# Gate/up as pairs of 64-row tiles that swap roles, in a segmented attention and feed-forward kernel

## The chip, the cores and the metric

The kernel runs on one core of a Trainium2 chip. The metric is the device time of one launch in microseconds (us). The engines of the core are named as in the profile: PE (TensorE, the matmul array) with PEld for its weight loads, DVE (VectorE), ACT (ScalarE), POOL (GpSimd), and SP, whose queue issues most of the transfers. A transfer issued by ScalarE stands on the queue ACTq.

## The reference

```python
xn = _layernorm(x)                       # x: 2048 x 448
# A: 16 heads of 28, 4 segments of 512 tokens, a memory M, z carried along
q, k, v = xn @ wq, xn @ wk, xn @ wv
for s in range(4):
    a_dot = softmax(qs @ ks.T * scale + mask) @ vs
    a_mem = (phi(qs) @ M) / (phi(qs) @ z + 1e-06)
    o = g * a_mem + (1 - g) * a_dot      # g = sigmoid(beta), one per head
    M, z = M + phi(ks).T @ vs, z + phi(ks).sum(rows)
s = o @ wo
# B: 448 -> 1792 -> 448
b = (gelu(xn @ w_gate) * (xn @ w_up)) @ w_down
out = x + s * silu(b)
```

`phi(t)` is `t + 1` for positive `t` and `exp(t)` otherwise.

## The kernel before

The work is cut into four segments of 512 tokens (four blocks of 128). The width 448 is three chunks of 128 and a rest of 64 rows; the 1792 hidden features are 14 chunks of 128 (`NFC`).

**A planner writes the order.** `fast_path` (L339) doesn't issue instructions at once. It makes a list of operations (`Op`, L26), each with its engine, a modelled duration, what it depends on (`deps`), what must have started before it (`after`), the buffers it takes (`acq`) and uses, and a priority. `arrange` (L276) plays them through on its model and sorts them by start. Each engine then executes its operations in that order. Priorities come from the table `PRIO` (L87); `STEP` (L258) says, for many operations, after which of the ten score steps of an attention they may start. Thus a change of these tables moves work on every engine, without changing the work.

**The array's modes.** The planner knows four modes of the array: full (128 rows), `r64` (two tiles of 64 rows), `r32` (four tiles of 32 rows, for the scores, L985) and `c32` (four tiles of 32 columns, for the product of probabilities and values, L1047). Tiles of one mode work side by side.

**Stages.** In order of time: normalisation of segment 0 and its projections; gate/up of segment 0 (G0); attention of segments 0 and 1 (A0, A1); G1; A2; G2; A3; G3; and the last down products (D3). The projections of later segments (L714), the down products (L1155), the memory's update and reads (L860, L898) and the output products (L1185) are fitted between the score steps.

**Gate/up** (`gate_up`, L1075). For each chunk of 128 hidden features the gate and the up product each need three full-array matmuls of 512 columns and one of 64 rows. The 64-row rests of both weights lie in one tile, `wh_sb`, gate in rows 0 to 63 and up in rows 64 to 127, so the two rests run side by side in `r64`. They are collected: `VISITS` (L1073) gives four visits a segment, in which the rests of up to four chunks are multiplied (L1104), with the full matmuls (L1089) of the chunks between the visits. Then ScalarE takes the gelu of the gate (L1114) and VectorE multiplies by the up product (L1119). A chunk holds two of the eight PSUM banks.

**Projections of later segments** (`project`, L801). Two blocks make a pair: six full matmuls as two operations (`Unit.full`, L721) and one visit in `r64` for the two 64-row rests (`visit`, L768), named `wr...`. The visit is tied to come before a given score step.

**The start** (`layer_norm(0)`, L603). All four blocks of x are centred (`xc`, L663), transposed by TensorE (L596) and evicted, and the projections of segment 0 are made from centred x; their eviction multiplies by the reciprocal width (L752, L754). The fully normalised x (L653) is transposed as well, for gate/up. ScalarE issues one x load and three loads of `wv` (L490) ahead of its first table load (L567).

**Other parts named below.** The phi exponentials of keys and queries (L826, `exwk..`, `exwq..`). The guard (L1239): squares of `wq` and `wk` (L1248), summed (L1251) into the tile `um`, one product (L1258), and comparisons; it says whether the fast path's softmax without a maximum was allowed. The same tile `um` takes the masked memory update of segments 1 and 2 (L872). The residual sum (L1176) is the last reader of x. `x_sb` has four buffers, one for each segment, `pt` (the probabilities) has five.

## Time and profile before

| | |
|---|---|
| runs, us | 229.61, 230.47, 435.18 |
| median of the runs, us | 230.47 |
| span of the profiled execution, us | 227.6 |
| mean granted clock of the array | 0.999 |
| G0 | 16.03 to 38.66 |
| A0 and A1 | 38.66 to 88.49 |
| G1 | 88.49 to 111.31 |
| A2 | 111.31 to 138.86 |
| G2 | 138.86 to 161.69 |
| A3 | 161.69 to 186.32 |
| G3 | 186.32 to 209.20 |
| D3 and the end | 209.20 to 227.60 |

The profiled execution's own time is its span of 227.6 us and what lies around it; the two lower runs are 2.0 and 2.9 us over that span. In the profile, "L1089" is line 1089 of the kernel; a group of instructions is given as output<-inputs, with partitions x elements, "x12" is the number of instructions, and an arrow in brackets names what ended the idle time before an instruction. `pp` and `ps` are PSUM banks. Starts are in us from the start of the span. Matmuls overlap, so the pitch of a row of matmuls is read from their starts or from a merged piece of the chain, not from the duration of one.

### The profile page before, as it was taken

The page shows a single profiled execution, that of the slowest core. Times are in us where ns is not written, and L with a number is a line of the kernel's source. Part 1 is how long each engine was busy: PE and PEld are TensorE (multiplying, and loading weights), DVE is VectorE, ACT ScalarE, POOL GpSimd, SP SyncE. Part 2 cuts the span into 40 slices and gives each one's busy share as a digit, 9 for nine tenths or more (in the row PEclk, how much of TensorE's full clock was granted, in tenths as well). Part 3 has the DMA queues.
Part 4 walks back from the last instruction along what each step waited for, and adds up shares of the span by engine and source line. Part 5 has one row for each costly group of instructions (what it writes and reads, how often), then busy time and mean ns, then how long its engine had stood idle before and what let it go on. Part 6 is the DMA issues. An engine that isn't in the chain of part 4 may idle for free.

```text
span 227.6 us, 4462 instructions
## 1 busy us (share of the span) xinstructions
PE 217.5 (96%) x1557; PEld 95.6 (42%) x1570; DVE 152.7 (67%) x287; ACT 152.7 (67%) x212; POOL 129.3 (57%) x221
## 2 busy tenths in 40 slices
PE   7999999889999999999999999999999999999991
PEld 2544433333544434344444444344444434444561
DVE  3799998767965795674875587863746463647262
ACT  4799645999898779432788898443878875346120
POOL 8601400579588599603599989853199477604500
PEclk9999999999999999999999999999999999999999
DMA  6999569964434763217603132272500018135011
GB/s 215 222 357 259 103 152 248 237 128 83 48 72 72 183 127 74 76 38 201 186 20 68 27 71 69 59 196 59 140 1 4 12 45 225 31 84 125 4 40 50
DMA packets 44708, 25.11 MB, mean 110 GB/s; under 512 B 30808, under 2 KB 40856, under 8 KB 44680
## 3 DMA queue, kind: packets, MB, share of 16 engines
q1 hardware_dynamic: 43704, 24.05, 44.7%
q10 hardware_dynamic: 976, 0.71, 1.0%
q8 instruction: 14, 0.23, 0.4%
q14 instruction: 14, 0.11, 0.2%
HBM read 16.00 MB, written 2.98 MB: 83 GB/s over the span
## 4 chain that ended last, share of the span: by engine, by line
PE 82%; ACT 10%; DVE 2%; issue 2%; ACTq 1%; POOL 1%; DVEq 0%; POOLq 0%
PE ps L1155 16%; PE ps L1089 15%; PE pp L1089 14%; PE ps L714 11%; PE pp L985 5%; PE ps L1185 5%; PE ps L1047 4%; ACT pt L1000 3%; PE ps L1104 3%; PE pp L1104 3%; PE pp L1155 2%; ACT pt L1248 2%; PE ps L898 1%; PE ps L860 1%; PE ps L1221 1%
## 5 line engine op out<-in xcount | busy, mean ns | idle before, releaser
L1000 ACT ACTIVATE pt<-pp 128x1024 bf16<-128x1024 f32 x75 | 73.3, 1037 | 11.8 <-PE pp L985 9.9
L1011 POOL TENSOR_SCALAR_AFFINE_SELECT pt<-pt 128x256 bf16<-128x256 bf16 x128 | 54.3, 448 | 26.0 <-ACT pt L1000 23.6
L1155 PE MATMUL ps<-wd_sb,hT 128*128 128x448 bf16 x182 | 39.0, 354 | 0.4 <-DVE qs L750 0.4
L1114 ACT ACTIVATE gl<-pp 128x512 bf16<-128x512 f32 x28 | 15.8, 595 | 29.0 <-PE pp L1104 23.2
L1155 PEld LDWEIGHTS <-hT 128*128 128x128 bf16 x210 | 18.8, 98 | 20.1 <-issue 5.0
L1119 DVE TENSOR_TENSOR hT<-gl,pp 128x512 bf16<-128x512 bf16 x28 | 18.4, 682 | 11.6 <-ACT gl L1114 11.5
L1119 DVE TENSOR_TENSOR hT<-gl,ps 128x512 bf16<-128x512 bf16 x28 | 18.7, 677 | 11.0 <-ACT gl L1114 8.4
L1114 ACT ACTIVATE gl<-ps 128x512 bf16<-128x512 f32 x28 | 16.6, 597 | 13.0 <-PE ps L1089 6.1
L1089 PEld LDWEIGHTS <-wu_sb 128*128 128x128 bf16 x168 | 16.4, 98 | 20.1 <-issue 0.3
L1089 PEld LDWEIGHTS <-wg_sb 128*128 128x128 bf16 x168 | 14.9, 98 | 22.5 <-issue 7.1
L909 POOL TENSOR_TENSOR om<-om,rb 128x512 f32<-128x512 f32 x12 | 14.9, 1268 | 15.9 <-DMA rb<-rdr 15.8
L714 PEld LDWEIGHTS <-xnT 128*128 128x128 bf16 (+1 forms) x192 | 15.0, 96 | 20.6 <-issue 10.1
L1089 PE MATMUL pp<-xnT,wu_sb 128*128 128x512 bf16 x84 | 22.7, 379 | 0.3
L1089 PE MATMUL ps<-xnT,wu_sb 128*128 128x512 bf16 x83 | 22.5, 379 | 0.2
L956 POOL TENSOR_TENSOR oT<-oa,om 128x512 bf16<-128x512 f32 x12 | 16.0, 1337 | 11.5 <-DVE oa L953 11.5
L1089 PE MATMUL ps<-xnT,wg_sb 128*128 128x512 bf16 x81 | 22.1, 380 | 0.3 <-issue 0.3
L1089 PE MATMUL pp<-xnT,wg_sb 128*128 128x512 bf16 x76 | 21.2, 380 | 0.4 <-issue 0.3
L831 POOL TENSOR_SCALAR e<-e 128x896 bf16<-128x896 bf16 (+1 forms) x12 | 12.8, 1070 | 10.9 <-ACT e L826 10.9
L985 PE MATMUL pp<-qT,kT 32*128 32x512 bf16 (+3 forms) x238 | 17.0, 301 | 2.0 <-ACT pt L1000 1.8
L646 POOL TENSOR_TENSOR rs<-rs,nhalf 128x1 f32<-128x1 f32 (+1 forms) x7 | 6.1, 882 | 16.1 <-DVE rs L641 16.1
L883 DVE COPY oa<-ps 128x512 f32<-128x512 f32 x16 | 10.9, 683 | 5.2 <-PE ps L1047 5.0
L1176 POOL TENSOR_TENSOR oo<-sg,x_sb 128x448 bf16<-128x448 f32 x12 | 12.4, 1037 | 2.7 <-DVE sg L1196 2.7
(121 smaller groups left out, 325.3 us busy)
## 6 DMA issues: line engine op xcount, KB each, us to landing
rb<-rdr SPq DMA_DIRECT2D x28, 256.0 KB
out_dram<-oo SPq DMA_DIRECT2D x15, 112.0 KB
wd_sb<-in_B_w_down_dram SPq DMA_DIRECT2D x2, 784.0 KB
x_sb<-in_A_x_dram SPq DMA_DIRECT2D x3, 448.0 KB
rdr<-dc SPq DMA_DIRECT2D x28, 32.0 KB
wg_sb<-in_B_w_gate_dram SPq DMA_DIRECT2D x2, 384.0 KB
wu_sb<-in_B_w_up_dram SPq DMA_DIRECT2D x2, 384.0 KB
wg_sb<-in_B_w_gate_dram SPq DMA_DIRECT2D x1, 576.0 KB
```

The source lines that it names most:

```text
L714: nc.tensor.matmul(out=self.bank.ap()[:, 0:D], lhsT=self.xT.ap()[r, c, n * P:(n + 1) * P], rhs=self.w[r, c, :], **kw)
L831: o = gps(f"mi{nm}{s}{half}", n / 1024, lambda: nc.gpsimd.tensor_scalar(out=t(), in0=t(), scalar1=1.0, scalar2=0.0, op0=ALU.min, op1=ALU.max),
L909: oU[s, g, 1] = t, gps(f"sm{s}{g}", 1.22, lambda t=t, r=r: nc.gpsimd.tensor_tensor(out=t.ap(), in0=t.ap(), in1=r.ap(), op=ALU.mult), deps= ...
L956: oT[s][1].append(gps(f"cb{s}{g}", 1.22, lambda g=g, t=t, tm=tm: nc.gpsimd.tensor_tensor(out=dst.ap()[:, g, :], in0=t.ap(), in1=tm.ap(), o ...
L985: nc.tensor.matmul(out=S2[i // 2].ap(i % 2)[:, c0:c0 + n], lhsT=kT[s][0].ap()[r, g, kb * P:(kb + 1) * P], rhs=qT[s][0].ap()[r, g, kb * P:L ...
L1000: nc.scalar.activation(out=dst, in_=src, func=ACT.Exp, scale=scale)
L1011: nc.gpsimd.affine_select(out=v, in_=v, pattern=[[0, 2], [1, P]], compare_op=ALU.is_ge, fill=0.0, base=0, channel_multiplier=-1)
L1089: nc.tensor.matmul(out=bf[fc].ap(i), lhsT=w[:, c, fc * P:(fc + 1) * P], rhs=xT.ap()[:, c, :], start=begins and c == 0, stop=not begins and ...
L1104: nc.tensor.matmul(out=bf[fc].ap(i), lhsT=wh_sb[r, fc * P:(fc + 1) * P], rhs=xT.ap()[r, NC3, :], start=fc in begins, stop=fc in ends)
L1114: a = act(f"ge{s}{fc}", L, lambda: nc.scalar.activation(out=gl.ap(), in_=bf[fc].ap(0), func=ACT.Gelu_apprx_tanh), func="gelu", deps=[o], a ...
L1119: nc.vector.tensor_tensor(out=hT[s][0].ap()[:, fc, :], in0=gl.ap(), in1=bf[fc].ap(1), op=ALU.mult), deps=[a] + held,
L1155: nc.tensor.matmul(out=bank.ap()[:, 0:D], lhsT=hT[s][0].ap()[:, fc, b * P:(b + 1) * P], rhs=wd_sb[:, fc, :], start=(fc == 0), stop=(fc == ...
```

## The change

Gate/up no longer uses the full array. Per chunk, `part(fc, 0)` multiplies gate weights of rows 0 to 63 and up weights of rows 64 to 127 of each of the three chunks, and the rests, as four pairs of 64-row tiles; `part(fc, 1)` swaps the roles in three pairs. Both tiles then write the other one's bank, and a tiny ScalarE activation (`ty`) between the two parts waits for both tiles of the first part and is waited for by both of the second. The order is: first part of chunk fc + 1, second part of chunk fc.

A projection pair is one operation `pj`, with its rests ahead or behind as the array's mode suggests (`flex`). In segment 0 only blocks 0 and 2 are projected from centred x (`EARLY`), the others from normalised x, and two keep-warm matmuls are added. The loads of the 64-row rests of `wv` move from ScalarE's queue to SP's. x has three buffers, so segment 3's x takes that of segment 0 after its last residual sum; `pt` has six. The masked update `um` depends on the guard. Phi exponentials of all segments may be tied to score steps, also to those of the attention before. `PRIO`, `STEP`, some modelled durations, and the choices of banks (`BANKS`) are new.

```diff
-        VISITS = (((), (0, 1)), ((2, 3), (4, 5)), ((6, 7), (8, 9)), ((10, 11), (12, 13)))
...
+            if rest:
+                prev = visit(f"wr2{s}", list(rest), at(ph, -1), after=[att.get("sc_end")])
+            def part(fc, turn):
                 nonlocal prev
 
                 def mm():
-                    for i, w in enumerate((wg_sb, wu_sb)):
-                        for c in range(NC3):
...
+                    for c in range(NC3 + 1 - turn):
                         for i in range(2):
...
+                            w = wh_sb if c == NC3 else (wg_sb, wu_sb)[i ^ turn][:, c, :]
+                            m = nc.tensor.matmul(out=bf[fc].ap(i ^ turn), lhsT=w[side[i], fc * P:(fc + 1) * P],
+                                                 rhs=xT.ap()[side[i], c, :], start=not turn and c == 0,
+                                                 stop=turn == 1 and c == NC3 - 1)
+                            if not turn:
+                                ended[fc, i] = m
+                            elif c == 0:
+                                ordered(m, turns[fc])
...
+                if not turn:
+                    def turn_over():
+                        turns[fc] = nc.scalar.activation(out=idle[0:1, :], in_=nhalf[0:1, 0:1], func=ACT.Identity)
+                        for i in range(2):
+                            ordered(turns[fc], ended[fc, i])
+                    swapped[fc] = op(f"ty{s}{fc}", {"ACT": (0.2, 0.25)}, turn_over, deps=[prev], after=[nhalf_in], prio=at(ph, fc) - 401)
...
+            part(0, 0)
+            for fc in range(NFC):
+                if fc < NFC - 1:
+                    part(fc + 1, 0)
+                h = part(fc, 1)
+                a = hidden(fc, h)
```

```diff
-        xs = tiles(NSEG, [P, NB, D], BF16, "x_sb")
+        x_p = slots(NSEG - 1, [P, NB, D], BF16, "x_sb")
+        xb = [Buf(x_p, [(s % (NSEG - 1),)]) for s in range(NSEG)]
...
-        pt_p = slots(5, [P, HG, L], BF16, "pt")
+        pt_p = slots(6, [P, HG, L], BF16, "pt")
...
-        wv_in = weight("ACT", "wv", wv_sb, A_wv)
-        wk_in = weight("SP", "wk", wk_sb, A_wk)
-        wq_in = weight("SP", "wq", wq_sb, A_wq)
+        wv_in = whole("ACT", "wv", wv_sb, A_wv)
+        wk_in = whole("SP", "wk", wk_sb, A_wk)
+        wv_in += rest("wv", wv_sb, A_wv)
+        wk_in += rest("wk", wk_sb, A_wk)
+        wq_in = whole("SP", "wq", wq_sb, A_wq) + rest("wq", wq_sb, A_wq)
...
-            out=igate[:, 0:1], in_=nhalf[:, 0:1], func=ACT.Exp), deps=[nhalf_in], after=wv_in, prio=-400)
+            out=igate[:, 0:1], in_=nhalf[:, 0:1], func=ACT.Exp), deps=[nhalf_in], after=wv_in[:1], prio=-400)
...
-                for b in range(NB):
+                for b in EARLY:
...
+                    o = turned_by_pe("c", b, [centred] + xc_z, cols, [], xcT[0], -905 + b)
+                    bank = Buf(B_, EIGHT)
+                    kept_warm.append(pe(f"wm{b}", [L], lambda bank=bank: nc.tensor.matmul(
+                        out=bank.ap(), lhsT=warm[:, 0:P], rhs=warm, start=True, stop=True), deps=[warm_in], after=[o],
+                        prio=-300 + b, acq=[bank]))
...
-                self.scaled = s == 0
+                self.scaled = s == 0 and n in EARLY
...
+                    first = o_of[us[0]].tail_first
+                    if first:
+                        tails(True)
+                    for u in us:
+                        for c in range(NC3):
+                            u.product(c, start=not first and c == 0, stop=first and c == NC3 - 1)
+                    if not first:
+                        tails(False)
...
-                    out=um[:], in0=uv(), in1=bd, op=ALU.mult), deps=[o, mem["acc"]], prio=pr - 400,
+                    out=um[:], in0=uv(), in1=bd, op=ALU.mult), deps=[o, mem["acc"], mem["ok"]], prio=pr - 400,
```

Of the tables, the prediction speaks of these entries: in `STEP`, `wo00`, `wo01`, `wo02`, `wo03` go from 10, 10, 10, 0 to 6, 7, 0, 7, and `exwk01` gets 1; in `PRIO`, `ty22` is 625 and `ge21` is 626 (the lower goes first).

More of the change, by code (lines that the diff above doesn't have):

```diff
@@ L807, in project, with mm, tails @@
                 us = [Unit(s, nm, n, -8400.0) for nm, n in pair]
[L808 to L813 removed]
+                def mm(us=us):
+                    def tails(first):
+                        for u in us:
+                            u.product(NC3, start=first, stop=not first)
+                    first = o_of[us[0]].tail_first
+                    if first:
+                        tails(True)
+                    for u in us:
+                        for c in range(NC3):
+                            u.product(c, start=not first and c == 0, stop=first and c == NC3 - 1)
+                    if not first:
+                        tails(False)
+                u, nm = us[0], pair[0][0]
+                new = not u.dst[2:] and nm != "wq"
+                ns = [D] * (2 * NC3 + 1)
+                occ = sum(n / 2400 + 0.0025 for n in ns) + SWITCH
+                o = op("pj{}{}{}".format(s, *pair[0]), {"PE": (occ, occ + 0.17)}, mm, mode="full", flex=True,
+                       deps=sum((x.needs(False) + x.needs(True) for x in us), []), prio=-8400.0,
+                       acq=[x.bank for x in us] + ([u.dst[0]] if new else []), uses=[u.xT], after=u.dst[2:3])
+                o_of[u] = o
+                if new:
+                    u.dst.append(o)
+                for x in us:
+                    x.out(o)
+                pairs_of.append((o, sc, k))
+        o_of, pairs_of = {}, []
         tabled, phis = [], []
@@ L1071, in fast_path, with ordered @@
         hT = {}
-        VISITS = (((), (0, 1)), ((2, 3), (4, 5)), ((6, 7), (8, 9)), ((10, 11), (12, 13)))
+        def ordered(later, earlier):
+            tc.add_manual_dep(later.ins, earlier.ins.name, mybir.DependencyInfo(
+                mybir.DependencyClass.Sync, mybir.DependencyReason.DATA), reason="one PSUM bank, two row tiles")
         def gate_up(s, ph, rest=()):
```

156 lines of the change are left out of this document (70 added, 86 removed), and 375 rows, old and new, of tables (BANKS, PRIO, STEP).

## The prediction

> **What bounds the kernel now.** I read the page first (busy shares, then the chain that ended last), then busy time by stage, then the chain in order of time, then the waits. The page:
>
> ```profile
> PE 217.5 (96%) x1557; PEld 95.6 (42%) x1570; DVE 152.7 (67%) x287; ACT 152.7 (67%) x212; POOL 129.3 (57%) x221
> PE 82%; ACT 10%; DVE 2%; issue 2%; ACTq 1%; POOL 1%; DVEq 0%; POOLq 0%
> ```
>
> TensorE is busy in 96% of the 227.6 us, and 82% of the chain that sets the end is TensorE. A busy TensorE isn't yet one at its peak, so the question is what its time consists of. By stage (gate/up of segment 0, attention of segments 0 and 1, gate/up of 1, of 2, of 3):
>
> ```profile
> core 0: us, PE busy (x) PEld busy (x) DVE busy (x) ACT busy (x) POOL busy (x), PEclk, DMA share, GB/s
> ...
> 16.03:38.66 22.63, 22.30 (x114) 8.91 (x115) 21.45 (x51) 15.01 (x24) 3.66 (x3) 1.00 0.89 197
> 38.66:88.49 49.83, 47.98 (x447) 20.87 (x447) 38.17 (x73) 44.70 (x56) 37.98 (x72) 1.00 0.61 117
> 88.49:111.31 22.82, 22.56 (x130) 9.30 (x132) 13.88 (x22) 11.15 (x18) 11.04 (x13) 1.00 0.47 122
> ...
> 138.86:161.69 22.83, 22.57 (x131) 9.22 (x132) 14.26 (x21) 11.56 (x18) 12.86 (x14) 1.00 0.42 115
> ...
> 186.32:209.20 22.88, 22.57 (x127) 9.49 (x130) 11.18 (x19) 11.15 (x17) 10.31 (x13) 1.00 0.44 118
> ```
>
> Each gate/up stage takes 22.6 to 22.9 us with TensorE full, at granted clock 1.00, and ScalarE half idle (11 to 15 us of about 23). Attention of segments 0 and 1 has both full: TensorE 47.98 and ScalarE 44.70 of 49.83. A piece of the chain in the last gate/up stage shows what the full TensorE spends:
>
> ```profile
> 196.69 2.59 PE pp L1089 x12
> 199.28 0.54 PE pp L1104 x4
> 199.82 0.43 PE ps L1104 x4
> 200.25 2.70 PE ps L1089 x12
> ```
>
> Twelve full-array matmuls of 512 columns take 2.59, so 0.216 each. Four 64-row matmuls take 0.43: two run at a time, and a pair costs 0.216 as well. The piece in which the array goes from full to 64 rows is 0.11 longer (0.54 against 0.43), and so is the one in which it goes back (2.70 against 2.59).
>
> **The change, part by part.** *Gate/up in 64-row tiles.* Per chunk of 128 features, before: six full matmuls and one 64-row pair, 7 slots of 0.216. After: four pairs, then three pairs, again 7 slots. The streaming is unchanged at 98 slots, 21.2 us per segment. What goes are changes of mode: four visits a segment (VISITS), entered three times from full matmuls and left four times to them, so 7 x 4 = 28 changes of 0.11: -3.1 us. Coming into and leaving the stage costs as before, and so does a probability product (1047) within it. The guard's one-row product (1258) is in full mode and may now stand within 64-row work: +0.1, one change more.
>
> *Twice the instructions.* 14 matmuls a chunk for 8, 336 more in all. The same visit seen matmul by matmul:
>
> ```profile
> 199.21 0.61 PE L1104 MATMUL pp<-xnT,wh_sb 64*128 64x512 bf16 x4
> 199.65 0.59 PE L1104 MATMUL ps<-xnT,wh_sb 64*128 64x512 bf16 x4
> ```
>
> The first two pairs take 0.44 from start to start, 0.01 more than 2 x 0.216, because the start after a change is a little long; nothing shows 98 pairs in a row. I take no cost. The upper end is that 0.01 on each of 392 pairs, +3.9. The lower end is 0, since no row has a 512-column slot under 0.216. The Trainium skill, "TensorEngine Tiling (Array Packing)", section "Instruction Overhead", speaks against my zero: each matmul is to have some 60 cycles of overhead. With 512 columns in 0.216 that is an estimated 25 ns, 336 x 25 ns = 8.4 us, and the sum would be about +5 in place of -3.4; by that rule the four matmuls of 0.43 would take 0.05 longer than two full ones, which they don't, so I weigh it little.
>
> *The swap.* Between the two turns of a chunk stands a tiny ScalarE activation that waits for both tiles and that the second turn waits for.
>
> ```profile
> L1104 PE MATMUL pp<-xnT,wh_sb x56: 376/376/387, 16.0 to 205.7; 64*128 64x512 bf16 x56
> ```
>
> ```profile
> 183.45 0.39 PE L985 MATMUL pp<-qT,kT 32*128 32x512 bf16 x4
> 183.94 1.94 ACT L1000 ACTIVATE pt<-pp 128x1024 bf16<-128x1024 f32 x2 [0.64 <-PE pp L985]
> 185.93 0.39 PE L985 MATMUL pp<-qT,kT 32*128 32x384 bf16 x6 [0.30 <-ACT pt L1000]
> 188.36 1.28 ACT L1114 ACT_TABLE_LOAD   x1
> ```
>
> ```profile
> 4.36 0.20 ACT L567 ACTIVATE igate<-nhalf 128x1 f32<-128x1 f32 x1
> 17.15 1.14 ACT L752 ACTIVATE hT<-ps,rs 128x448 bf16<-128x448 f32 x2
> 36.82 0.60 ACT L1114 ACTIVATE gl<-ps 128x512 bf16<-128x512 f32 x1
> ```
>
> Its path: 0.16 for the matmul's tail (0.376 against a 0.216 slot), 0.10 from TensorE to ScalarE (183.84 to 183.94), 0.20 for the activation, 0.05 back (185.88 to 185.93): 0.51. Its cover: the second turn of the chunk before and the first of the chunk after, 7 slots, 1.51; 0.86 at the first chunk and 0.65 at the last. A gelu of 0.60 in front makes 1.11, still inside; an exponential (0.97 each in the row of two) about fits; a table load of 1.28 would be 0.28 too late, and that comes once at a stage's head. Cost taken: 0; ends 0 and 3 x 0.28 = +0.8 (a systematic wait is a rival below). 56 x 0.20 is 11 us more on ScalarE, 2.8 per stage that has 8 to 12 free. Identity costs no table load beside exponentials (17.15 follows one directly); beside gelus no row shows it. The Trainium skill, "ScalarE: Activation LUTs", section "Table sets", counts identity as a filler of every set; without that each swap would reload twice and nothing here would hold.
>
> *Gelu later.* Until now a chunk's gate product was complete three slots before its up product; now both end together, so the last gelu, the table load behind it and the first exponentials of the next attention come up to 0.65 later. *A phi exponential* of segment 0 (exwk01) is now held until the first scores, which takes 0.95 into the stage where ScalarE leads the chain:
>
> ```profile
> 22.00 0.95 ACT L826 ACTIVATE e<-kn 128x896 bf16<-128x896 bf16 x1
> 43.41 5.74 ACT pt L1000 x8
> PE pp L985 <- ACT pt L1000: 1.8, 3, 1.0
> ```
>
> There TensorE waits 1.8 us. Against it stand a sixth pt buffer and newly ordered work. Ends: all 1.8 gone, or 0.65 + 0.95 = 1.6 more. I take +0.3, near zero and on the side of the two mechanisms that I can see. After the later gate/up stages other matmuls cover it.
>
> *The start.*
>
> ```profile
> 1.33 1.70 ACTq L490 DMA_DIRECT2D wv_sb<-in_A_wv_dram  x3
> 3.06 1.28 ACT L567 ACT_TABLE_LOAD   x1 [3.06 <-issue]
> 4.46 0.56 ACT L615 ACTIVATE hT<-x_sb 128x448 bf16<-128x448 bf16 x1
> 5.58 1.05 ACT L598 COPY xnT<-ps 128x512 bf16<-128x512 bf16 x2
> 6.20 0.74 PE L714 MATMUL ps<-wv_sb,xnT 128*128 128x448 bf16 x3 [0.20 <-ACT xnT L598]
> 6.78 0.39 PE L596 MATMUL ps<-oT,hT 128*128 128x128 bf16 x4
> 7.00 0.39 PE L596 MATMUL pp<-oT,hT 128*128 128x128 bf16 x4
> 9.73 0.74 PE L714 MATMUL pp<-wk_sb,xnT 128*128 128x448 bf16 x3
> ```
>
> ScalarE issues three weight loads before its table load; two of them move to SP's queue, so its statistics and the first eviction come up to 1.1 earlier (two thirds of 1.70), and the first product at 6.20 with them. Two groups of four transposes go (0.22 each, 6.78 to 7.00): -0.44; two keep-warm matmuls come: +0.43. But only two blocks can now be projected early; the other two need their width first, and the key weights, which were used from 9.73, stand no earlier. SP issues the same two tails later, ahead of wq. Ends -1.1 and +0.5; I take -0.4.
>
> *Projection pairs as one piece, tails first or last.* A tail costs a change of 0.11 in and one out either way; only where a full product followed the tail, and scores preceded the piece, is one saved. Of 18 pairs I count that for a few: -0.3, ends -0.6 and +0.6 (the uninterrupted piece is 1.4 long and can hold scores up).
>
> *Three x buffers.* x of segment 3 now loads only after segment 0's last residual sum. *Guard:* `um` of segment 1 waits for the guard.
>
> ```profile
> 113.30 1.04 POOL L1176 TENSOR_TENSOR oo<-sg,x_sb 128x448 bf16<-128x448 f32 x1 [2.41 <-DVE sg L1196]
> 116.72 1.43 PE ps L714 x8
> 31.98 0.38 PE L1258 MATMUL ps<-um,ones 128*1 128x128 f32 x2
> 78.82 0.68 DVE L872 TENSOR_TENSOR um<-ps,bdmask 128x512 f32<-128x512 f32 x1
> ```
>
> The guard has 47 us of room: nothing. For x, a residual sum of segment 0 stood at 113.30 and segment 3's first products at 116.72, so the old order would be too late; the new steps put `wo00`, `wo01`, `wo03` after score step 6 or 7 of segment 1 (before: 10, 10, 0), some 20 us before. The load, norm and four transposes then lie in gate/up of segment 1, where VectorE is busy 13.88 of 22.82. Cost 0; if it is late, up to two product pairs of 1.43 leave attention 2 for a place among 64-row work: +0.4 for four changes, and SP's later loads of reciprocals wait behind it.
>
> Sum: -3.1 + 0.1 + 0.3 - 0.4 - 0.3 = -3.4, a span of 224.2. The runs shown are 229.61 and 230.47 (the median), 2.0 to 2.9 over the span of 227.6; with the middle, 2.45, the time is 226.7.
>
> **The rivals.** *The whole replan works* (A): the start gains its 1.1, the pairs 0.6, the waits on exponentials 1.0: -3.0 - 1.1 - 0.6 - 1.0 = -5.7, 224.4. For it: those are the only other losses on a full TensorE. Against: ScalarE at 44.70 of 49.83 leaves little. *The gain is given back in attention* (B): stages 0 and 1 get 1.6 more and pairs cost 0.6 more: -3.0 + 2.2, 229.3. For it: ScalarE's load there and the later gelu. *The swap waits* (C), the slower side: a swap queued on ScalarE behind the gelu of the chunk before, which itself waits for that chunk's second turn, comes 0.65 + 0.16 + 0.10 + 0.60 + 0.20 + 0.05 = 1.76 after its first turn against a cover of 1.51, so TensorE stands 0.25. At 14 of 56 chunks the gain is gone; at 30 the time is 226.7 + 7.5 = 234.2. Against it: the listed priorities put ty22 (625) ahead of ge21 (626). *The pace falls* (D): 0.01 more on every pair, +3.9, 230.6. For it: no row has more than four pairs in a row. Against it: within those four the pace is back to 0.216 after the first.
>
> **How the numbers follow.** Forecast 0.48, A 0.27, B 0.09, C 0.10, D 0.06. The forecast's own range is 225.0 to 228.3. The range 223.5 to 231.5 takes in A, B and D and leaves out most of C. Two per cent is 4.6 us, about what a measurement of this kernel can tell from no change: faster means under 225.9, which holds most of A and the low edge of the forecast, 0.30; slower means over 235.1, which is C with 34 or more late swaps, 0.08; the rest, 0.62, lies within.
>
> **What would show it.** Right: four gate/up stages of about 22.0 us without full-array matmuls, the two turns 0.86 and 0.65 long, no wait of TensorE for the tiny activation; the first value product before 6.0. Wrong: a wait of a gate/up product on ScalarE in the list of waits (C); 28 matmuls of two chunks taking over 3.05 (D); a longer chain through the exponentials after 40 us (B); segment 3's first products after 125 us (x late).

## The result and the profile after

The changed kernel ("after") takes 231.58 us in the median against 230.25 for the kernel before in the same rounds, a ratio of 1.0068 with a 95% interval of 1.0045 to 1.0091. It is a little slower (0.7%, and the interval is only 0.5 us to either side), where 226.7 was forecast; the time lies 0.1 above the top of the range. Ratios below are all to the kernel before, run on the same chip, and leave disturbed executions out. The profiled execution has a span of 230.1 us, 2.5 more than before. The medians differ by 1.3 only: a run lasts 1.7 to 1.9 us longer than its own span, so the profiled execution of before was about 0.9 faster than its median run, and that of after about 0.3 slower. The stage differences below are those of two single executions. First the page's busy shares and the shares of its chain:

```profile
PE 218.5 (95%) x1899; PEld 99.8 (43%) x1900; DVE 156.7 (68%) x282; ACT 164.5 (71%) x272; POOL 127.0 (55%) x221
PE 66%; DVE 12%; ACT 7%; DMA 6%; issue 4%; POOL 3%; SPq 2%; DVEq 0%; ACTq 0%
```

TensorE is still busy 95% of the span, but its share of the chain has fallen from 82% to 66%, and VectorE's has risen from 2% to 12%. That second line is the first hint. The windows by stage (start, G0, A0 and A1, G1, A2, G2, A3, G3, the end) say where:

```profile
0.00:17.12 17.12, 14.93 (x82) 6.71 (x84) 10.79 (x28) 10.68 (x22) 8.30 (x34) 1.00 0.87 263
17.12:39.03 21.91, 21.60 (x198) 9.67 (x194) 19.44 (x47) 16.76 (x39) 1.65 (x2) 1.00 0.79 152
39.03:88.98 49.95, 48.34 (x432) 20.91 (x432) 36.67 (x63) 45.69 (x60) 37.85 (x71) 1.00 0.54 112
88.98:113.49 24.51, 23.31 (x229) 11.59 (x228) 20.82 (x32) 14.55 (x32) 15.90 (x19) 1.00 0.47 120
113.49:141.69 28.20, 27.58 (x235) 12.28 (x234) 21.04 (x34) 23.54 (x28) 20.87 (x36) 1.00 0.41 76
141.69:163.62 21.93, 21.93 (x217) 9.70 (x212) 12.56 (x20) 13.62 (x31) 10.06 (x13) 1.00 0.47 125
163.62:188.71 25.09, 24.90 (x212) 10.80 (x210) 16.24 (x28) 21.27 (x25) 18.42 (x35) 1.00 0.11 29
188.71:210.64 21.93, 21.93 (x219) 9.70 (x212) 10.60 (x18) 13.20 (x30) 8.62 (x11) 1.00 0.43 120
210.64:230.10 19.46, 13.95 (x102) 8.42 (x100) 8.49 (x17) 5.18 (x11) 5.30 (x4) 0.94 0.10 29
```

Against the kernel before, the stages differ by: start +1.1 (17.12 against 16.03), G0 -0.7, A0 and A1 +0.1, G1 +1.7, A2 +0.7, G2 -0.9, A3 +0.5, G3 -0.9, end +1.1; together +2.5. In G2 and G3 TensorE is busy for all of 21.93 us, the 22.0 that the prediction named. The gain is there in three of the four gate/up stages. It is lost at the start, in G1, A2 and A3, and at the end.

That the swap costs nothing is seen in a piece of G0's chain and in the list of TensorE's waits:

```profile
30.27 1.51 PE ps L1146 x14
31.78 1.51 PE pp L1146 x14
```

```profile
PE ps L1146 <- DVE oa L936: 1.2, 2, 1.0
PE pp L744 <- ACT kn L783: 0.5, 1, 0.5
PE pp L1146 <- ACT nhalf L1158: 0.3, 1, 0.3
```

Fourteen matmuls of a chunk, seven pairs, take 1.51, so 0.216 a pair over whole stages. The tiny activation (`nhalf`, L1158) is waited for once, 0.3 us. The longest wait inside gate/up is another: for VectorE's copies `oa` (L936).

### The profile page after: what moved, and what is told of

Same layout as the page of the kernel before. It is cut to its first block, busy times and chain, and to the rows that moved or that the text cites. A ratio compares the mean times of both kernels' runs of the same rounds, so it can differ in the third digit from the quotient of the medians.

```text
span 230.1 us, 5179 instructions
## 1 busy us (share of the span) xinstructions
PE 218.5 (95%) x1899; PEld 99.8 (43%) x1900; DVE 156.7 (68%) x282; ACT 164.5 (71%) x272; POOL 127.0 (55%) x221
## 4 chain that ended last, share of the span: by engine, by line
PE 66%; DVE 12%; ACT 7%; DMA 6%; issue 4%; POOL 3%; SPq 2%; DVEq 0%; ACTq 0%
PE ps L1206 14%; PE ps L1146 13%; PE pp L1146 10%; PE ps L744 10%; PE pp L1038 4%; PE ps L1100 3%; PE ps L1236 3%; DVE hT L1172 3%; DMA rb<-rdr 2%; PE pp L744 2%; DMA x_sb<-in_A_x_dram 2%; ACT pt L1053 2%; DVE dc L973 2%; PE ps L597 2%; POOL pt L1064 1%
## 5 line engine op out<-in xcount | busy, mean ns | idle before, releaser
L1053 ACT ACTIVATE pt<-pp 128x1024 bf16<-128x1024 f32 x72 | 70.5, 1034 | 12.3 <-PE pp L1038 10.3
L1064 POOL TENSOR_SCALAR_AFFINE_SELECT pt<-pt 128x256 bf16<-128x256 bf16 x128 | 52.2, 437 | 15.8 <-ACT pt L1053 15.2
L1146 PE MATMUL ps<-xnT,wu_sb 64*128 64x512 bf16 x180 | 47.7, 376 | 0.2 <-DVE oa L936 0.2
L1146 PE MATMUL ps<-xnT,wg_sb 64*128 64x512 bf16 x180 | 46.1, 376 | 1.0 <-DVE oa L936 1.0
L1206 PE MATMUL ps<-wd_sb,hT 128*128 128x448 bf16 x196 | 42.2, 353 | 0.8 <-DVE om L936 0.5
L1146 PE MATMUL pp<-xnT,wu_sb 64*128 64x512 bf16 x156 | 41.7, 376 | 0.3 <-ACT nhalf L1158 0.3
L1146 PEld LDWEIGHTS <-wu_sb 64*128 64x128 bf16 x336 | 30.6, 94 | 21.4 <-ACT nhalf L1158 2.4
L1146 PE MATMUL pp<-xnT,wg_sb 64*128 64x512 bf16 x156 | 39.8, 376 | 0.0
L1146 PEld LDWEIGHTS <-wg_sb 64*128 64x128 bf16 x336 | 30.1, 94 | 19.5 <-issue 1.9
L744 PEld LDWEIGHTS <-xnT 128*128 128x128 bf16 (+1 forms) x192 | 15.2, 96 | 22.4 <-issue 10.6
L1158 ACT ACTIVATE nhalf<-nhalf 1x1 f32<-1x1 f32 x56 | 11.1, 198 | 16.1 <-PE ps L1146 10.1
L936 DVE COPY oa<-ps 128x512 f32<-128x512 f32 x16 | 10.7, 680 | 6.9 <-PE ps L1100 6.3
```

The costliest lines, as they stand in the source:

```text
L744: nc.tensor.matmul(out=self.bank.ap()[:, 0:D], lhsT=self.xT.ap()[r, c, n * P:(n + 1) * P], rhs=self.w[r, c, :], **kw)
L1053: nc.scalar.activation(out=dst, in_=src, func=ACT.Exp, scale=scale)
L1064: nc.gpsimd.affine_select(out=v, in_=v, pattern=[[0, 2], [1, P]], compare_op=ALU.is_ge, fill=0.0, base=0, channel_multiplier=-1)
L1146: m = nc.tensor.matmul(out=bf[fc].ap(i ^ turn), lhsT=w[side[i], fc * P:(fc + 1) * P], rhs=xT.ap()[side[i], c, :], start=not turn and c == ...
L1158: turns[fc] = nc.scalar.activation(out=idle[0:1, :], in_=nhalf[0:1, 0:1], func=ACT.Identity)
L1206: nc.tensor.matmul(out=bank.ap()[:, 0:D], lhsT=hT[s][0].ap()[:, fc, b * P:(b + 1) * P], rhs=wd_sb[:, fc, :], start=(fc == 0), stop=(fc == ...
```

## Three places to look at

**G1: one short VectorE instruction.** VectorE's rows in G1, then GpSimd's of the same time:

```profile
90.44 4.00 DVE L973 TENSOR_SCALAR dc<-dc,igate 128x64 f32<-128x64 f32 x1 [0.74 <-DMA dc<-den]
94.48 0.55 DVE L977 RECIPROCAL dc<-dc 128x64 f32<-128x64 f32 x1
94.95 1.22 DVE L936 COPY oa<-ps 128x512 f32<-128x512 f32 x2
```

```profile
90.04 2.21 POOL L1064 TENSOR_SCALAR_AFFINE_SELECT pt<-pt 128x256 bf16<-128x256 bf16 x6
92.21 1.28 POOL L928 TENSOR_TENSOR macc<-macc,um 128x512 f32<-128x512 f32 x1
93.44 0.95 POOL L884 TENSOR_SCALAR e<-e 128x896 bf16<-128x896 bf16 x1
94.52 1.03 POOL L1227 TENSOR_TENSOR oo<-sg,x_sb 128x448 bf16<-128x448 f32 x1
```

The same multiply of a 128x64 tile takes 0.25 in the median of its seven executions. Here it takes 4.00, from 90.44 until just after GpSimd's run without a gap ends at 94.39. In before the longest of the seven takes 0.41:

```profile
69.26 0.41 DVE L920 TENSOR_SCALAR dc<-dc,igate 128x64 f32<-128x64 f32 x1 [0.98 <-DMA dc<-den]
```

Both end 0.05 after the end of a GpSimd instruction: in before of the next mask, in after of the last instruction of the run. Theory 1 is that VectorE's multiply is held by GpSimd's run. Reciprocal and copies stand behind it in VectorE's order, and the copies free the PSUM banks that gate/up needs. In TensorE's rows (start, duration, and in brackets the idle time before):

```profile
91.45 1.57 PE L1100 MATMUL ps<-pt,vaug 128*32 128x512 bf16 x32
...
94.27 0.38 PE L1146 MATMUL ps<-xnT,wg_sb 64*128 64x512 bf16 x1
95.63 0.37 PE L1146 MATMUL ps<-xnT,wg_sb 64*128 64x512 bf16 x1 [0.98 <-DVE oa L936]
96.22 0.37 PE L1146 MATMUL ps<-xnT,wu_sb 64*128 64x512 bf16 x1 [0.22 <-DVE oa L936]
```

From 94.27 to 96.22 two slots of 0.216 take 1.95, so 1.5 is lost. Also late behind it is the rest of this chain on SP's queue, and with it the load of segment 3's x, in SP's rows:

```profile
101.31 0.58 SPq L586 DMA_DIRECT2D x_sb<-in_A_x_dram  x1
```

**The start: copies that wait for another matmul.** Two keep-warm matmuls (L699), a key product (L744) and the copies (L623) of transposed blocks out of PSUM, from TensorE's, ScalarE's and VectorE's rows of after:

```profile
5.07 0.63 PE L699 MATMUL pp<-oT 128*128 128x512 bf16 x1
8.54 0.73 PE L744 MATMUL pp<-wk_sb,xnT 128*128 128x448 bf16 x3
9.79 0.74 PE L744 MATMUL pp<-wk_sb,xnT 128*128 128x448 bf16 x3 [0.30 <-DVE xnT L623]
```

```profile
5.74 0.58 ACT L623 COPY xnT<-pp 128x512 bf16<-128x512 bf16 x1 [0.78 <-PE pp L699]
10.57 0.59 ACT L623 COPY xnT<-pp 128x512 bf16<-128x512 bf16 x1 [1.47 <-PE pp L744]
```

```profile
9.31 0.42 DVE L623 COPY xnT<-pp 128x512 bf16<-128x512 bf16 x1 [0.72 <-PE pp L744]
```

Each copy begins 0.04 after the end of a matmul that wrote something else: 5.74 after 5.07 + 0.63, 9.31 after 8.54 + 0.73, 10.57 after 9.79 + 0.74. What they share is a `pp`, a tile of two PSUM banks. The change lets the start use both halves (`EIGHT`, before `END`), and theory 2 is that the program that is built orders accesses by tile, not by half.

**The end: ScalarE's jump.** After the last store all engines jump over the slow path. ScalarE's jump and its first instruction behind it, in the rows of that line before, and after (count, durations in ns, first and last start):

```profile
L1704 ACTq COMPARE_BRANCH  x1: 76/76/76, 224.7 to 224.7; - x1
L1704 ACTq EVENT_SEMAPHORE  x1: 17/17/17, 225.2 to 225.2; - x1
```

```profile
L1756 ACTq COMPARE_BRANCH  x1: 68/68/68, 226.5 to 226.5; - x1
L1756 ACTq EVENT_SEMAPHORE  x1: 17/17/17, 229.2 to 229.2; - x1
```

Before, 0.42 us lie between the two; after, 2.66. Of the fourteen kernels traced for this case nine have such a slow jump, and in each of them the span ends 0.96 after that first instruction; in the five with a fast jump it ends 2.4 to 3.8 after it, so something else comes last there. The time from the last matmul's start to the end grows from 4.9 to 5.7.

## The experiments

All of them keep the planned order and move or change single operations of it: `at_` finds an operation by name, `move` puts it behind (or ahead of) another.

**The multiply on ScalarE** (dg_scalar).

```diff
+            o.turned = lambda: nc.scalar.activation(
+                out=dc.ap(), in_=dc.ap(), func=ACT.Identity, scale=igate[:, side:side + 1], bias=ones[:])
...
+                nc.vector.memset(ones[:], 1e-6)
...
+        at_["dg11"].fn = at_["dg11"].turned
+        move(["dg11"], "exwk21")
```

> After, with one instruction on another engine: the multiply of the memory's denominators of segment 1 by the gate (dc, 128x64, 4.00 us on VectorE at 90.44 in after) is an activation on ScalarE, put behind ScalarE's exp of kn at 90.23; the 1e-6 is added behind the factor instead of ahead of it. The planned order of everything else is kept. Theory 1 (VectorE's multiply stood for as long as GpSimd ran back to back, 90.04 to 94.39, and the copies, products and DMA issues behind it stood with it): the TensorE gaps of 1.15 and 0.38 us at 94.26 to 96.22 go, G1 falls from 24.51 to 22.9 to 23.2, the load of segment 3's x is issued at about 97.5 instead of 101.31, and the time falls by 1.3 to 2.0 us to 229.6 to 230.3. Rival (G1 is late for other reasons: its first products are behind the last attention products, and the evacuations would be late in any case): G1 stays at 24.3 to 24.7 and the time at 231.3 to 231.8.

Measured: 230.16 us, ratio 0.9997 (0.9965 to 1.0028), 0.7% under after. The profiled execution, with 228.33, is the fastest of its runs. The windows of G1 and A2:

```profile
88.28:111.06 22.78, 22.78 (x229) 10.23 (x228) 17.31 (x33) 14.77 (x33) 15.85 (x19) 1.00 0.52 135
111.06:137.93 26.87, 26.87 (x234) 12.14 (x233) 19.27 (x32) 23.48 (x28) 21.26 (x36) 1.00 0.44 78
```

TensorE is full in both, G1 is 1.73 shorter, and segment 3's x is issued at 98.35. Theory 1 holds as far as the cost goes: it was this multiply that held G1 up. A2 is 1.3 shorter as well; the next runs show that this isn't owed to the earlier x.

**The multiply behind the evacuations** (dg_behind).

```diff
+        move(["dg11", "rc11", "rd110", "rd111"], "ou130")
```

> After, with the same multiply left on VectorE but put behind the two evacuations of the attention accumulators (oa) that stood behind it in VectorE's order, its reciprocal and the first two DMAs with it. Theory 1: the multiply still stands until GpSimd's run ends (over 1 us instead of 0.25), but the evacuations are out by about 92, so TensorE's two gaps of 1.53 in all fall to under 0.4 and G1 to 23.1 to 23.5; what is behind the multiply on SyncE's queue stays late, so the load of segment 3's x stays at about 101 and A2 gains nothing: 230.2 to 230.6. Rival (G1 late for other reasons): 231.3 to 231.8 and G1 at 24.5.

Measured: ratio 1.0054 (1.0011 to 1.0096), G1 23.53. The stand of 1.5 is gone and the multiply takes 0.71, but TensorE waits 0.6 elsewhere in G1 for VectorE's hidden features, and x is issued at 101.93. G1 gives 1.0, the least that was expected, and the whole time shows no gain (the interval overlaps that of after): what is put off is late for someone else.

**PSUM places at the start** (banks_apart).

```diff
+        for name, place in {"wm0": 7, "wm2": 7, "wk02": 2, "wk01": 0}.items():
+            next(b for b in at_[name].acq if b.pool is B_).slots = (place,)
+        move(["evwk01"], "evwk03", before=True)
```

> After, with the order kept and four PSUM places at the start changed: the two keep-warm matmuls and two key products no longer write the other half of the two-bank tile that a transposed block is still to be copied out of (one eviction of keys moved ahead of another for it). Theory 2 (a copy out of one half waits for the matmul that was written into the other half meanwhile: the copies began 0.04 us after that matmul's end, at 5.74, 6.35, 9.31 and 10.57): the copies begin at about 5.3, 6.0, 8.8 and 9.6, the first value product at about 5.9 instead of 6.38, and the first gate/up matmul comes 0.3 to 0.8 us earlier than 17.12; time 230.8 to 231.3. Rival (the start waits for block 2's normalised x behind the memset of wo_sb, 9.55 to 11.15, alone): the first gate/up matmul stays at 17.0 to 17.2 and the time at 231.3 to 231.8, although the copies come earlier.

Measured: ratio 1.0000 (0.9961 to 1.0040). The copies, then the first gate/up matmul:

```profile
5.32 0.59 ACT L623 COPY xnT<-pp 128x512 bf16<-128x512 bf16 x1 [0.48 <-PE pp L621]
9.85 0.58 ACT L623 COPY xnT<-pp 128x512 bf16<-128x512 bf16 x1 [0.43 <-PE pp L621]
```

```profile
16.17 0.38 PE L1146 MATMUL pp<-xnT,wg_sb 64*128 64x512 bf16 x1
```

The copies now wait for the transposes alone, and the first gate/up matmul comes 0.95 earlier. The first value product does not: it was expected at 5.9 and comes at 6.71, and the last 0.31 of its wait is for `wv`, two of whose loads the change moved to SP's queue:

```profile
6.71 1.30 PE L744 MATMUL ps<-wv_sb,xnT 128*128 128x448 bf16 x6 [0.31 <-DMA wv_sb<-in_A_wv_dram]
```

So the start is read in two pieces. From the first value product to the first gate/up matmul it takes 9.46 us here, 10.74 in after (6.38 to 17.12), 9.83 before (6.20 to 16.03). In all seven kernels here with these places apart it is 9.46 to 9.92, in the six others that have after's start 10.74 to 11.17. Theory 2 holds, and is worth 1.3 in this piece. At the first matmul of G1 about 0.7 of it is left (it comes at 88.3 against 89.0 in the median of these kernels, full_rows left out), so part of it is lost again on the way there. In this run the multiply in G1 was also quick, though GpSimd ran beside it:

```profile
90.02 0.46 DVE L973 TENSOR_SCALAR dc<-dc,igate 128x64 f32<-128x64 f32 x1 [0.70 <-DMA dc<-den]
```

Here it began 4 ns after a mask instruction had begun and ended with that mask; in after it began 43 ns after one. What decides is not shown: at 180.07 of this same run it began 54 ns after a mask, and it got in behind that mask too (0.40). G1 was 22.78 and x was issued at 98.82, nearly as early as with the multiply on ScalarE, yet A2 took 28.17. So the early x isn't what shortened A2 there.

**The memset of `wo_sb`** (memset_early).

```diff
+        at_["wo0"].fn = lambda: nc.vector.memset(wo_sb[:], 0.0)
+        move(["wo0"], "warm")
```

> After, with the order kept but for one instruction: the memset of wo_sb (1.60 us on GpSimd at 9.55) is made by VectorE before the first x lands, where VectorE was idle from 1.20 to 3.25. The theory that the memset held block 2's normalised x (1.62 us instead of 0.40): it takes 0.40, its transposes come at about 12.4 instead of 13.53, and the first gate/up matmul 0.4 to 0.8 us earlier; time 230.8 to 231.2. Rival (the waits of the copies for matmuls of the other half bank, theory 2, set the start alone): the first gate/up matmul stays within 0.15 us of 17.12. If both are needed, neither this kernel nor the one with the banks apart gains more than 0.3.

Measured: ratio 1.0051 (0.9997 to 1.0105), 10.82 from the first value product to the first gate/up matmul (5.99 to 16.81). The first gate/up matmul comes 0.31 earlier than in after, but the first value product is 0.39 earlier already, so nothing is gained between them. The rival was right in that, by VectorE's row and then TensorE's:

```profile
9.34 0.39 DVE L679 TENSOR_SCALAR xn<-x_sb,mv,rs 128x448 bf16<-128x448 bf16 x1
```

```profile
13.21 0.40 PE L621 MATMUL ps<-oT,xn 128*128 128x128 bf16 x4
14.06 0.73 PE L744 MATMUL pp<-wq_sb,xnT 128*128 128x448 bf16 x3 [0.45 <-ACT kn L783]
```

The normalised x takes 0.39 instead of 1.62, and nothing comes of it: its transposes stand behind key products in TensorE's order. A stall of 1.2 us that looked like a cause was none.

**The price of a mode change** (full_rows).

```diff
+                    for i in range(0 if turn else 2):
+                        ended[fc, i] = nc.tensor.matmul(out=bf[fc].ap(i), lhsT=wh_sb[side[i], fc * P:(fc + 1) * P],
+                                                        rhs=xT.ap()[side[i], NC3, :], start=True, stop=False)
+                    for c in range(NC3):
+                        m = nc.tensor.matmul(out=bf[fc].ap(turn), lhsT=(wg_sb, wu_sb)[turn][:, c, fc * P:(fc + 1) * P],
+                                             rhs=xT.ap()[:, c, :], start=False, stop=c == NC3 - 1)
+                        if turn and c == 0:
+                            ordered(m, turns[fc])
```

> After, with the same planned order, the same number of matmul slots (7 of a 512-column pair or single for each of the 56 tiles) and the swap activations left in, but the three row blocks of gate and up as 128-row matmuls (the gate's three in a tile's first part, the up's three in its second) and only the 64-row rest as a pair, ahead of the gate's three: two changes between 64 and 128 rows in each tile, 112 in all, where after has next to none. Mode theory (0.11 us for a change, the price of the prediction's first term): 12.3 us more, each gate/up stage from 21.7 to about 24.8, the time at 242 to 246. Rival (after's gate/up is faster through its form, and a change costs nothing by itself): 231 to 233.

Measured: 244.54 us, ratio 1.0607 (1.0535 to 1.0679). The two late gate/up stages, in which TensorE is full:

```profile
149.17:173.86 24.69, 24.69 (x135) 8.74 (x128) 13.17 (x21) 13.47 (x33) 10.03 (x13) 1.00 0.49 120
198.72:223.41 24.69, 24.69 (x136) 8.84 (x129) 10.90 (x18) 13.14 (x32) 8.60 (x11) 1.00 0.37 101
```

24.69 - 21.93 = 2.76 for 28 changes, 0.099 each, though this kernel has 8 matmuls a chunk for 14. That the whole time fits the expectation is partly chance: G0 grew by 2.15 only, and in G1 the multiply stood 7.20 us and TensorE 4.3 with it. The Trainium skill, "TensorEngine Tiling (Array Packing)", section "Key Properties", says that a change of mode drains TensorE; a cost at each change agrees with that, and these stages give its size; the drain itself is not seen in them.

**The jump told of later** (hint_later).

```diff
-        near = next(k for k, o in enumerate(order) if o.name == "sc30")
+        near = next(k for k, o in enumerate(order) if o.name == "sc37")
```

> After, with one thing moved: the place where ScalarE and VectorE are told of the jump at the kernel's end (ahead of segment 3's eighth scores instead of its first). In after ScalarE runs 112 instructions between the two (86 before), and its first instruction behind the jump comes 2.66 us after it (0.42 before). Theory 3 (what was fetched for the jump is gone after so many instructions): the 2.66 falls to about 0.4 to 0.5 and the time from the last matmul's start to the end of the span from 5.71 to 4.9, as before: 0.8 us less, 230.5 to 231.0. Rival (the last store's landing sets the end, and lands as late in any case): 5.6 to 5.9 and 231.3 to 231.8.

Measured: 231.75 and 232.30 us (two runs, no interval). Span 230.6, 5.85 from the last matmul's start to the end, 2.75 for the jump, with 83 instructions in between. full_rows, with 108 in between, had 0.42. Theory 3, too many instructions, fell. The end of 5.85 is what the rival forecast, but its reason isn't seen: here, too, the span ends 0.96 after the first instruction behind the jump.

**The mends together** (mended: three of the edits above; mended_oa: and the multiply of `oa` in A2 moved).

```diff
+        move(["ca13"], "evwq31")
```

> After with three mends together: the PSUM places of the start apart, segment 1's multiply of the memory's denominators on ScalarE (1e-6 added behind the factor), and the jump told of later. If the three losses are what they seem (start 1.3, G1 1.7, end 0.8) and add up: 3.8 us less than after, 227.0 to 228.5, ratio to before 0.985 to 0.993; A2 may give up to 1.3 more. Rival (what is won ahead of A2 is waited for again in attention, whose chain of exps and of VectorE sets its end): 229.0 to 230.5.

> The three mends, and in A2 the multiply of an attention accumulator (oa by rb, two inputs in SBUF, 0.68 us alone and 1.74 us beside GpSimd's masks in two of the runs so far) behind two evacuations of queries and the memory's read that stood behind it on VectorE. If VectorE's waits for GpSimd also cost A2 (28.4 against 27.1 us): A2 at 27.0 to 27.4 in every run, up to 0.8 us less than the three mends alone, 226.5 to 228. Rival (the evacuations are not what A2 waits for): the same as the three mends alone within 0.3.

Measured: mended 228.69 us, ratio 0.9924 (0.9892 to 0.9955); mended_oa 227.83, 0.9875 (0.9831 to 0.9919). The first lies between its two forecasts: its start is 15.42, 1.7 shorter than in after, but A0 and A1 take 50.77, 0.8 longer. The intervals of the two overlap; A2 tells them apart. The multiply of `oa` and the window of A2, in mended, then in mended_oa:

```profile
122.80 1.75 DVE L1008 TENSOR_TENSOR oa<-oa,rb 128x512 f32<-128x512 f32 x1
```

```profile
110.88:138.96 28.08, 27.67 (x235) 12.32 (x234) 21.09 (x33) 23.48 (x28) 20.88 (x36) 1.00 0.40 72
```

```profile
124.77 0.91 DVE L1008 TENSOR_TENSOR oa<-oa,rb 128x512 f32<-128x512 f32 x1
```

```profile
111.05:137.81 26.76, 26.76 (x236) 12.05 (x234) 18.88 (x31) 23.57 (x28) 20.96 (x36) 1.00 0.44 77
```

Where this multiply takes 1.74 or 1.75 (after, banks_apart, mended), A2 takes 28.1 to 28.2 and TensorE stands for the copies behind it. Where it takes 0.76 (dg_scalar), or stands behind those copies (mended_oa), A2 takes 26.8 to 26.9 with TensorE full; pad_24 below, with the multiply moved too, has 27.3. It isn't the masks that hold it, as the expectation had it, but GpSimd's addition `oT`, here in mended, then in dg_scalar:

```profile
122.73 1.27 POOL L1011 TENSOR_TENSOR oT<-oa,om 128x512 bf16<-128x512 f32 x1
```

```profile
122.88 1.70 POOL L1011 TENSOR_TENSOR oT<-oa,om 128x512 bf16<-128x512 f32 x1
```

In after, banks_apart and mended the multiply begins 0.07 to 0.08 behind this addition and ends 0.55 after it. In dg_scalar it begins 0.18 ahead of it (122.69), and it is the addition that takes longer, 1.70 for 1.27. The planner does mark this multiply as one that can't run beside GpSimd; in the runs the two met all the same.

**The jump again** (mended_jump: told of 8 us ahead of the end; pad_24 and pad_40: told of as in after, with 24 and 40 idle activations in ScalarE's stream; mended_pads: 24 of them where ScalarE waits anyway).

```diff
+                for _ in range(n):
+                    nc.scalar.activation(out=idle[0:1, :], in_=nhalf[0:1, 0:1], func=ACT.Identity)
```

> The kernel with the three mends and the multiply of oa moved (mended_oa), but with the place where ScalarE and VectorE are told of the jump put 8 us ahead of the end, behind ScalarE's next to last silu of segment 3, instead of ahead of the eighth scores. Number of instructions between the two fell as the cause (83 of them as slow as 112, and 108 in another kernel fast). What the slow kernels have alone is a fetch of 8 KB of instructions 8.2 to 9.5 us ahead of the end. Theory 3b (that fetch of what follows in order takes the place of what had been fetched for the jump): told of behind it, ScalarE's first instruction behind the jump comes 0.4 to 0.6 us after it instead of 2.7, the time from the last matmul's start to the end falls from 5.8 to 4.9 to 5.3, and the time by 0.5 to 0.9 to 226.9 to 227.4. Rival (the jump is slow through where its target lies, told of or not): 5.8 as before, 227.6 to 228.0.

> The kernel mended_oa with the jump told of where after tells of it (segment 3's first scores), and 24 one-element activations put into ScalarE's stream in its idle 4.4 us ahead of segment 3's third silu; they do nothing but move what follows 24 instructions further. ScalarE's jump is slow (2.7 us) with 442 to 444 instructions ahead of it and fast (0.42) with 345 and 419, whenever it is told of. Theory 3c (what counts is where the end of ScalarE's stream falls in the 8 KB pieces in which it is fetched: slow when a new piece is entered some 16 instructions, 8.3 us from the end, ahead of the jump): entered 40 instructions ahead, the jump is fast, and the time from the last matmul's start to the end falls from 5.8 to about 4.9 to 5.3; 226.9 to 227.4. Rival (the jump is slow from some number of instructions on, 442 here): 2.7 again, end 5.8, 227.6 to 228.2.

> The same with 40 of them (24 ahead of the third silu, 16 ahead of the second), so that ScalarE's jump has 56 instructions of its last piece ahead of it. Theory 3c: fast, 0.4 to 0.5, end 4.9 to 5.3. Rival (slow from some number of instructions on): 2.7, end 5.8. If one of the two is fast and the other slow, the place decides, but not by the rule of theory 3c.

> The kernel mended_oa with 24 one-element activations as in pad_24, but laid into three waits of ScalarE that hold them (0.23 us each: 4, 6 and 14 of them ahead of segment 3's first, second and third silu, where it stood 1.51, 2.12 and 4.37 us). In pad_24 they took 5.6 us in the 4.4 us wait and the silu came 1.2 us late. Theory 3c: the jump is fast (0.43) and nothing is late, the time from the last matmul's start to the end falls from 5.8 to 4.9 to 5.3, and the time to 226.8 to 227.5, ratio to before 0.983 to 0.988. Rival (something else behind the last store sets the end): 5.6 to 5.9 with a fast jump, 227.6 to 228.2.

Measured: mended_jump 228.22, 0.9918 (0.9889 to 0.9948), jump 2.74 and end 5.83, so theory 3b fell too, and VectorE's jump, told of as late, rose from 0.52 to 2.99. pad_24 229.08, 0.9952 (0.9926 to 0.9977), and pad_40 230.22, 1.0005 (0.998 to 1.003): both jumps took 0.43. So it isn't a number of instructions from which on the jump is slow (468 and 484 ahead of it are fast, 442 to 444 slow). That the place where the stream ends decides, as theory 3c has it, fits these runs; that its pieces of 8 KB are the reason is not shown. The time didn't fall, because the fillers took 0.23 us each, more than the waits held. Spread out, in mended_pads:

```profile
L1781 ACTq COMPARE_BRANCH  x1: 68/68/68, 222.6 to 222.6; - x1
L1781 ACTq EVENT_SEMAPHORE  x1: 17/17/17, 223.1 to 223.1; - x1
```

227.57 us, 0.9844 (0.9775 to 0.9912). The kernel before spread from 229.49 to 232.65 in these rounds, so this ratio is the least sure; against 230.1 to 230.4, its medians in the other rounds, it would be 0.988 to 0.989. The 0.26 by which the time is under mended_oa's is not told apart from none by the runs. The profiles show more: up to the last matmul that of mended_pads is mended_oa's to within 0.1 us (it starts at 220.49 and 220.51), and the end is 5.30 instead of 5.82. The two kernels differ in the place of the announcement too, which made no difference in hint_later. A fetch of 8 KB of instructions, which the expectations name as a mark of the slow kernels, stands 8.92 us ahead of the end here as well, beside a fast jump.

The stages of the three kernels in us, each from one execution:

| | before | after | mended_pads |
|---|---|---|---|
| start | 16.03 | 17.12 | 16.31 |
| G0, G1, G2, G3 | 22.63, 22.82, 22.83, 22.88 | 21.91, 24.51, 21.93, 21.93 | 21.91, 22.78, 21.93, 21.94 |
| A0 and A1, A2, A3 | 49.83, 27.55, 24.63 | 49.95, 28.20, 25.09 | 50.05, 26.75, 25.08 |
| end | 18.40 | 19.46 | 19.05 |
| span | 227.6 | 230.1 | 225.8 |

## Why the prediction was wrong, step by step

**Gate/up, -3.1: right.** G0, G2 and G3 give 0.72, 0.90 and 0.95 for a forecast of 0.77 each. G1 without its stand is 22.78, level with before, but it holds 32 probability products where before had 16 (1.57 us for the row of 32 in the G1 rows above), about 0.8 of work that came over from A1. The 0.11 for a change measured 0.099. The 0.1 for the guard's product did not arise there: in after the product stands in A0 and A1.

**Twice the instructions, 0: right.** Seven pairs take 1.51 throughout. The overhead of some 60 cycles a matmul that the Trainium skill states ("TensorEngine Tiling (Array Packing)", section "Instruction Overhead") isn't seen as added time; rival D, 0.01 on each pair, is out too.

**The swap, 0: right.** One wait of 0.3 in 56. Rival C did not occur.

**The start, -0.4: the step failed.** It counted transposes, keep-warm matmuls and loads, and took the waits among them as unchanged; the start is 1.1 longer. The choice of banks, which is in the change as `EIGHT` for `END` and which the prediction passed over, cost 1.3. The moved loads helped less than assumed, too: the prediction named the first value product before 6.0 as a sign. It came at 6.38, behind a copy that waited for a keep-warm matmul, and in four of the seven kernels with the banks apart it stood for `wv` instead (0.20 to 0.77). With the banks apart the piece from the first value product on is 0.37 shorter than before (9.46 against 9.83). That this is about the forecast is luck: the whole start is no shorter (15.42 to 16.31, median 16.17, in these seven against 16.03).

**"x buffers and guard, 0, VectorE is busy 13.88 of 22.82": the step that cost most.** The work of normalising segment 3 did fit. But busy time was taken for the only thing VectorE can lack. What the change brought into G1 is a multiply in the middle of GpSimd's run of masks, add and minimum; the planner doesn't mark this multiply as one that can't run beside GpSimd, and the step had neither a place nor a price for it. Before gave a hint (0.41 for 0.25) but no row in which it was held for longer. It cost 1.73. (The load of x itself was not late by the prediction's own sign: segment 3's first product comes at 123.45, ahead of 125.) The Trainium skill, "SBUF — State Buffer", section "Who interferes with whom", has the rule: a `tensor_scalar` from SBUF to SBUF can take the port that VectorE shares with GpSimd, whoever is first has it for its whole instruction, and the other is blocked. The runs agree that it blocks. On how long, they agree in 21 of the 25 cases in which the multiply took over 0.3: it was held to the end of the GpSimd instruction under way or of the next. They differ in four, all in G1: in after it was held not for one instruction of 0.4 but for all five masks left and the two operations behind them, 4.00 us. What decides between the two stays open.

**Attention, +0.3 and -0.3: not settled.** A2 came out at +0.65, and at -0.7 to -0.8 where VectorE was not held. What the new pairs are worth can't be read from it, because work moved between the stages: A2 has twelve output products fewer than before and one projection pair more, by before's rows (0.76 for four products, 1.43 for a pair) 0.85 less. A3 with +0.46 has four output products more, 0.76. A0 and A1 came out at +0.1 with about 0.7 less work by the same rows, and took 49.7 to 51.1 in ten other kernels that have after's gate/up; what they lose to was not taken apart.

**The end: no step at all.** It is 1.1 longer. ScalarE's jump explains 0.5 of it, since that is what mended_pads gained; the 56 swap activations are among what moved the end of ScalarE's stream (442 instructions ahead of the jump, 345 before). Why the place decides stays open: the runs show that it goes with the length of the stream and not with the distance of the announcement, and nothing in them shows what happens in those 2.7 us.

Had the start (1.3), G1 (1.7), A2 (1.3) and the jump (0.5) not been lost, after's span would be 225.3, a little over the forecast 224.2. That is a sum and not a run; mended_pads, the nearest run, has 225.8.

**From span to time, +2.45: mis-sized.** Every run whose span is on record lasts 1.7 to 1.9 longer than that span. The prediction set the span of one execution against the times of others; with 1.76, as in after's profiled run, its time would have been 226.0, further from the 231.58.

## What to carry to other kernels

Price a replanned order not only by engine time and data dependences: look for short VectorE instructions that now fall into long gapless runs of GpSimd, and ask what is queued behind them, since a 0.25 us instruction can stand for the length of the run. When tiles are given new buffers, check which accesses then share one tracked tile, because halves of one tile order each other. And a stall is not yet a loss: move it away and see, as with the memset, before you build on it.

## What the hardware showed that was not expected

- A VectorE multiply of a 128x64 tile, 0.25 us by itself, took over 0.3 in 25 executions in these fourteen traces, and in each it ended 0.05 after the end of a GpSimd instruction. In 21 it was held to the end of the instruction under way or the next (0.33 to 0.71 in all), in four past six to ten instruction ends (3.96 in hint_later, 4.00 in after, 4.05 in memset_early, 7.20 in full_rows). A reciprocal of the same tile took 0.55 beside GpSimd's masks as well as alone (90.83 in dg_scalar).
- A VectorE multiply of two 128x512 tiles in SBUF, 0.68 by itself, and a GpSimd addition of two such tiles: whichever began second took longer (1.74 to 1.75 for the multiply in after, banks_apart and mended, 1.70 for 1.27 for the addition in dg_scalar).
- A jump that had been announced took ScalarE 0.42 to 0.44 or 2.66 to 3.19 us, and which of the two followed the length of its instruction stream (fast with 345, 419, 468 and 484 instructions ahead, slow with 442 to 444), not the distance of the announcement.
- The first value product came at 5.84 to 6.42 in kernels with the same instructions up to there (dg_scalar, full_rows, after, dg_behind, hint_later). Four transposes ahead of it took 0.39 in some and up to 0.63 in others, with a granted clock of 1.00 in the rows of all of them; why is not shown.
